# Row work of an attention kernel cut into four pieces, four more row maxima in its lead-in, and first rows on two queues

## The chip, the cores and the metric

One Trainium2 chip, one of its cores. The metric is the device time of one execution in microseconds (us). The engines are named as in the profile: PE (TensorE, the matmuls), PEld (TensorE's weight loads), DVE (VectorE), ACT (ScalarE), POOL (GpSimd) and SP (SyncE, which issues most DMAs).

## The reference

The input x has 2048 rows of 512. It is normalized, goes through multi-query attention (32 heads of 16 that share one k and one v) and, beside that, through two dense layers with Mish between them; the result is x plus their gated product.

```python
xn = _layernorm(x, axis=-1)
q = (xn @ wq).reshape(B, S, H, Dh).transpose(0, 2, 1, 3)      # S = 2048, H = 32, Dh = 16
k, v = xn @ wk, xn @ wv                                       # one key and value head
p = softmax(einsum("bhqd,bkd->bhqk", q, k) * Dh ** -0.5)
s = einsum("bhqk,bkd->bhqd", p, v).reshape(B, S, H * Dh) @ wo
h = einsum("bsd,df->bsf", xn, w1) + b1                        # F = 1792
g = silu(einsum("bsf,fd->bsd", h * tanh(softplus(h)), w2))
return x + s * g
```

## The kernel before, in words

**Steps.** The attention is 32 groups (v) of queries and heads, each against 16 blocks of 128 keys: 512 steps, step s being block s % 16 of group s // 16. A step makes four score products (`e`, L1090), four exponentials of them on ScalarE (`pts`, L1095) and, two steps later, eight products of these with the values into the bank `pv` (L1176). Since the softmax subtracts each query's maximum, a step also makes four products `m` (L1118) of a later group's queries, the other way round, so that VectorE can take their maxima along the free axis (L1122, into the table `mb`). These run LEAD = 20 steps ahead; 64 of them, 32 for each of two sides (a = 0 and 1), make up a group. The last 20 steps have none, and are run in ten pairs (`tail_pair`).

**Row work.** When both sides' counters `m_next` have reached `m_need(v)`, that is 32 * (v + 1), `top_rows` takes up the row work of group v, which `c_rows` (L1134) defines as four functions: `reduce` (L1141, the maximum over the four key chunks), `parts` (L1144 and L1146, the maximum's split into two numbers), `turn` (L1153, four transposes of 32 by 32) and `move` (two DMAs, L1162). These bring the maxima as two more rows into the queries' tile `qt`, where the score products of step 16 v and later read them. The functions stand in a queue, `rowq`, as three pieces: reduce, parts, turn with move. After each step `top_rows(1)` takes one piece; after a step that evacuated a bank on VectorE (`evacs[0]`) none, after each half of a unit two, after a pair three.

**Dense work.** PE's remaining time goes to the projections and the two dense layers, group by group: 12 or so accumulating products into a bank `xps`, each cut into two half-height products (L122) of which one side runs beside the other side's attention products. In `waves` (L619) a step takes k = 6, 4 or 8 of them, or none; below these are called w6, w4, w8 and w0 steps. A group of 13 to 16 products runs as a unit (`unit`, L684): four steps in two halves, each half with 16 half products, eight e, eight m and two steps' pv products (16). `unit_ready` opens one only at a step divisible by 4, and only when each item that the group reads is ready by the planner's clock; for a weight that comes last it grants a slack, `g.most`, of 0.5 steps there and of 2 elsewhere. Weights arrive by DMA and are split by POOL into a high and a low part (`wbs`, L170 and L175). The order on every engine is fixed when the program is built, from such estimates; at run time the engines only wait on semaphores.

**Banks.** In PSUM `e` has three banks, `m` three, `pv` one and `xps` one.

**Lead-in.** Before step 0, a planner loop (L1453 to L1575) places load, normalization, projections and the first maxima as tasks with estimated costs. It makes 2 * LEAD = 40 maxima per side, then group 0's row work, whose DMAs set `cdone`, the time at which the rows are expected in `qt`. Until 0.4 us before that time PE is given dense products, or, where no group is ready, products that nobody reads (`keep_warm`, L1431).

Of the kernel before, what the change touches and what calls it, by code (L numbers as in the profile page):

```python
# [20 lines left out]
P = 128  # L21
# [12 lines left out]
LEAD = 20  # L34
# [94 lines left out]
def block_kernel(ctx: ExitStack, tc: tile.TileContext, x, wq, wk, wv, wo, w1, b1, w2, out):  # L129
# [1004 lines left out]
    def c_rows(v):  # L1134

        mp = sb.tile([P, 2, 3, 8], F32R, tag="mp", name=f"mp{v}", bufs=2)
        mx = f(mp[:, :, 0])
        w = {}

        def reduce():  # L1140
            dve.reduce_max(out=mx, in_=mb_of[v].rearrange("p b (a z) -> p a z b", a=2), axis=AX.X)  # L1141

        def parts():
            dve.tensor_reduce(out=mp[:, :, 1], in_=mx.rearrange("p a (z o) -> p a z o", o=1), axis=AX.X,  # L1144
                              op=ALU.max, negate=True)
            dve.tensor_reduce(out=f(mp[:, :, 2]), in_=f(mp[:, :, 0:2]).rearrange("p a s z -> p a z s"), axis=AX.X,  # L1146
                              op=ALU.add, negate=True)

        def turn():
            cr = w["cr"] = sb.tile([32, P], F32, tag="cr", name=f"cr{v}", bufs=2)  # L1150
            for b in range(4):
                z = slice(32 * b, 32 * b + 32)
                dve.transpose(cr[:, z], f(mp[z, :, 1:3]).rearrange("p a s z -> p a (s z)"))  # L1153

        def move():
            q, cr = qt_of[v], w["cr"]
            if not lead:
                sp_t[0] = max(sp_t[0], us_of(step[0]) + 4.0)
            for a in range(1, -1, -1):
                r = 64 * a + 48  # L1160
                sp_at(0.68)
                sp.dma_start(f(q[r:r + 2]).rearrange("o p (t n) -> o (p t) n", n=P), cr[16 * a:16 * a + 16])  # L1162
        return reduce, parts, turn, move

    def pv(s):
# [268 lines left out]
    pick = [None, None]  # L1434

    def m_ready(t):
        if min(m_next) >= 2 * LEAD:
            return None

        def ready(v, n, a):  # L1440
            i = 2 * (n % 8 // 4) + a
            if len(qready.get(v) or ()) <= i or n // 8 not in kready:
                return 1e9
            return max(t, qready[v][i], kready[n // 8][a])
        r = []
        if m_next[0] == m_next[1]:
            free = m_ends[(-3, -5)[len(mseq) % 2] if 15 in xp_of else -2]
            s = [max(free, *(ready(v, got[v], a) for a in range(2))) if got[v] < 32 else 1e9 for v in range(2)]
            v = int(s[1] + 0.6 < s[0])
            r.append((s[v], (0, 1), (v, got[v])))  # L1450
        else:
            e = mseq[m_next[1]]
            r.append((max(ready(*e, 1), m_ends[-3]), (1,), e))  # L1453
        if m_next[0] < 4:
            r.append((max(ready(0, got[0], 0), m_ends[-3]) + 0.05, (0,), (0, got[0])))
        z, pick[0], pick[1] = min(r, key=lambda z: z[0])
        return z if z < 1e8 else None
# [17 lines left out]
    while True:  # L1475
# [19 lines left out]
        if not any(o[1] == "ACT" and o[0] < T["ACT"] + 0.1 for o in opts):  # L1495
            opts.append((T["ACT"], "ACT", "J"))
        s, e, k = min(opts, key=lambda o: o[0])
        if cdone[0] is not None and s >= cdone[0] - 0.4 and min(m_next) >= 2 * LEAD:
            break
        when(s)  # L1500
        for tag in items:
# [1 line left out]
        if k == "M":  # L1503
            d = max(T["DVE"], s + 0.45)
            for a in pick[0]:
                if m_next[a] == len(mseq):
                    mseq.append(pick[1])
                    got[pick[1][0]] += 1
                m_one(a)
                d += 0.6  # L1510
                m_ends.append(d)
            T["DVE"] = d
            T["PE"] = s + (0.25 if kind[0] == "M" else 0.45)
            kind[0] = "M"
            if vdone[0] == 0 and got[0] == 32 and m_next[0] == m_next[1]:
                vdone[0] = 1
                r = c_rows(0)
                r1 = task("DVE", 1.2, lambda: (r[0](), r[1](), r[2]()))

                def move():  # L1520
                    r[3]()
                    cdone[0] = now[0] + 2 * 0.65 + 2.0
                task("SP", 1.3, move, [r1])
        elif k == "X":
            fresh = cur["g"] is None
            if cur["g"] is not None or not waiting and (vdone[0] or begun[0] < 1 + (s - 18) / X_US) and begin():
                begun[0] += fresh
                fill(3)
                T["PE"] = s + 0.23 * 3 + (0.2 if kind[0] == "M" else 0)
                kind[0] = "X"  # L1530
            else:
                keep_warm()
                T["PE"] = s + 0.25
                kind[0] = "X"
        elif k == "J":
            tag = next((g for g in ("wq", "ws", "wb") if not any(soon(k, s) for k in plan["POOL"]) and arrived(g) and busy[0] + E0 < s + (4.5 if g == "ws" else 0.5)), None)
            n = ran[0]
            if tag:
                split(tag)
                T["ACT"] = s + 0.6  # L1540
            else:
                gap[0] = 0
                if not plan["POOL"]:
                    act_jobs(1)
                T["ACT"] = s + (0.65 if ran[0] > n else 0.15)
        else:
            plan[e].remove(k)
            if k.fill and cur["g"] is not None and s < 27.0:
                fill(1)
            elif k.fill and cur["g"] is None and not waiting:  # L1550
                keep_warm()
            k.fn()
            T[e] = max(s, T[e]) + k.us + (0.15 if e == "PE" and kind[0] == "M" else 0)
            k.end = T[e]
            if e == "PE":
                kind[0] = "T"
# [9 lines left out]
    rowq = deque()  # L1566
    skip = [0]

    def top_rows(n):
        if vdone[0] < 8 * NC and min(m_next) >= m_need(vdone[0]):  # L1570
            r = c_rows(vdone[0])
            rowq.extend([r[0], r[1], lambda r=r: (r[2](), r[3]())])
            vdone[0] += 1
        for _ in range(min(n, len(rowq))):
            rowq.popleft()()  # L1575

    def unit_ready(s):
        if cur["g"] is not None or cur["chunk"]:
            return False
        for g in queue:  # L1580
            g.most = 0.5
        due(s)
        ok = begin()
        for g in queue:
# [89 lines left out]
    for s in range(NS + 2000):  # L1674
        inm = s < NS - LEAD
        if s < skip[0]:
            continue
        if s % 4 == 0 and s + 4 <= NS - LEAD and unit_ready(s):
            for h in range(2):
                unit(s, h)  # L1680
                top_rows(2)
                evacs[0] = 0
                pump()
            base[:] = s + 4, us_of(s) + UNIT_US
# [2 lines left out]
        if inm or cur["chunk"]:  # L1687
# [2 lines left out]
            h = s % 2  # L1690

            def em(k):
                n = m_sides(1 - h, k // 2) if inm else 0
                x = deque(lambda i=i: e_one(s, i) for i in range(4))
                y = deque(lambda: m_one(1 - h) for _ in range(n))
                r = [[], []]
                for op in FEW if k == 4 else EM:
                    if op == "M" and y:
                        r[1 - h].append(y.popleft())
                    elif op == "E":  # L1700
                        r[1 - h].append(x.popleft())
                r[h] = [lambda: m_one(h) for _ in range(4 - n if inm else 0)]
                return r

            if s >= 2 and (s - 1) % 16 == 0 and s > 1:
# [8 lines left out]
        elif TAIL <= s < NS:  # L1714
            due(s)
            tail_pair(s)
            top_rows(3)
            evacs[0] = 0
            base[:] = s + 2, us_of(s) + PAIR_US
            pump()  # L1720
# [11 lines left out]
            due(s + 0.5)  # L1732
            fill(16)
        step[0] = s
        top_rows(0 if evacs[0] else 1)
        evacs[0] = 0
        base[:] = s + 1, us_of(s) + K_US.get(halves[0], STEP_US)
        pump()
# [14 lines left out]
```

## Time and profile before

| | |
|---|---|
| median of 3 runs | 1565.14 us (1565.11 to 1565.82) |
| the profiled execution | 1565.04 us, of which its span 1563.2 us |
| PE busy | 1551.0 us, 99% |
| DVE busy | 1366.9 us, 87% |
| ACT busy | 1295.0 us, 83% |
| POOL busy | 637.8 us, 41% |
| granted TensorE clock | 1.00 over the span |

The profile shows one execution. The span runs from its first to its last recorded instruction; the execution's time is 1.8 us longer. A busy share is an engine's busy time over the span: it does not tell what the engine that is behind waits for, which the chain of waits does.

### The profile page before, as it was taken

The numbers are of one execution on the slowest core, as the hardware profiler recorded it, in microseconds if no ns is written. First come the engines' busy times: TensorE is split into PE (matmuls) and PEld (weight loads), VectorE is DVE, ScalarE is ACT, GpSimd is POOL, SyncE is SP. The second block draws the span as 40 slices with busy tenths as digits, with TensorE's granted clock in tenths as the row PEclk, the third lists the DMA queues.
The fourth block names the chain that finished last, engine by engine and source line by source line (L and its number), as shares of the span: only waits on it lengthen the run. The fifth ranks groups of instructions, "written<-read, shape, count | busy, mean of one in ns | idle before, by whom it ended". The sixth has DMA issues, their size and how long they took to land.

```text
span 1563.2 us, 31137 instructions
## 1 busy us (share of the span) xinstructions
PE 1551.0 (99%) x11722; PEld 862.5 (55%) x11722; DVE 1366.9 (87%) x2376; ACT 1295.0 (83%) x2509; POOL 637.8 (41%) x668
## 2 busy tenths in 40 slices
PE   9999999999999999999999999999999999999998
PEld 6545655555455565565555556556554555565654
DVE  7988888888989988898999998898889999889945
ACT  6599888779888788877989788798798887879786
POOL 5788339437348121440543424054044232404213
PEclk9999999999999999999999999999999999999999
DMA  6343123224131313112214231222321223121021
GB/s 205 110 140 125 39 85 127 68 85 139 59 120 56 105 32 112 58 33 91 64 31 139 78 93 30 76 81 86 97 60 32 87 69 111 31 86 45 8 75 42
DMA packets 68498, 125.46 MB, mean 80 GB/s; under 512 B 15262, under 2 KB 29900, under 8 KB 68348
## 3 DMA queue, kind: packets, MB, share of 16 engines
q1 hardware_dynamic: 67916, 122.68, 24.7%
q8 instruction: 93, 1.52, 0.4%
q10 hardware_dynamic: 432, 0.79, 0.1%
q14 instruction: 57, 0.47, 0.1%
HBM read 75.57 MB, written 26.21 MB: 65 GB/s over the span
## 4 chain that ended last, share of the span: by engine, by line
PE 97%; DVE 2%; ACT 1%; DMA 0%; issue 0%; SPq 0%; DVEq 0%
PE xps L122 44%; PE pv L1176 32%; PE m L1118 11%; PE e L1090 6%; PE xps L118 1%; DVE mb L1122 1%; PE wop L122 0%; PE kp L356 0%; PE xp L315 0%; DMA pts<-in_dram 0%; ACT pts L1095 0%; PE y2ps L122 0%; PE warm L1431 0%; PE wop L118 0%; DVE cr L1153 0%
## 5 line engine op out<-in xcount | busy, mean ns | idle before, releaser
L1122 DVE TENSOR_REDUCE mb<-m 128x1 f32<-128x512 f32 x2048 | 1265.6, 682 | 152.2 <-PE m L1118 118.3
L1095 ACT ACTIVATE pts<-e 128x512 f32<-128x512 f32 x2048 | 1065.6, 605 | 220.1 <-PE e L1090 162.4
L1118 PE MATMUL m<-ks,qt 48*128 48x512 f32 (+1 forms) x2048 | 846.1, 424 | 1.7 <-DVE mb L1122 1.4
L1090 PE MATMUL e<-qt,ks 64*128 64x512 f32 x2048 | 752.1, 407 | 0.4 <-ACT pts L1095 0.4
L1176 PE MATMUL pv<-pts,vaug 128*32 128x512 f32 x4096 | 530.1, 603 | 0.0
L1118 PEld LDWEIGHTS m<-ks,qt 48*128 48x128 f32 (+1 forms) x2048 | 371.3, 185 | 91.3 <-DVE mb L1122 54.0
L1090 PEld LDWEIGHTS e<-qt,ks 64*128 64x128 f32 x2048 | 376.0, 186 | 26.7 <-ACT pts L1095 12.9
L122 PE MATMUL xps<-wbs,act 64*128 64x512 f32 x1270 | 324.0, 399 | 0.1
L122 PE MATMUL xps<-xt,ws 64*128 64x512 f32 x1128 | 312.3, 409 | 1.0 <-ACT pts L1095 1.0
L122 PEld LDWEIGHTS xps<-xt,ws 64*128 64x128 f32 x1128 | 194.3, 185 | 184.9 <-ACT pts L1095 123.2
L122 PEld LDWEIGHTS xps<-wbs,act 64*128 64x128 f32 x1270 | 227.3, 184 | 97.2 <-ACT pts L1095 26.8
L1176 PEld LDWEIGHTS pv<-pts,vaug 128*32 128x32 f32 x4096 | 88.1, 108 | 151.5 <-issue 143.9
L185 POOL TENSOR_SCALAR t<-t 128x512 f32<-128x512 f32 x56 | 34.5, 616 | 274.3 <-ACT t L814 274.3
L175 POOL TENSOR_TENSOR hb<-hb,t 128x512 f32<-128x512 f32 x56 | 72.2, 1289 | 120.7 <-ACT t L827 76.0
L122 PE MATMUL xps<-xt,wq 64*128 64x512 f32 x336 | 93.1, 409 | 0.0
L122 PEld LDWEIGHTS xps<-xt,wq 64*128 64x128 f32 x336 | 57.9, 185 | 55.0 <-ACT pts L1095 36.9
L122 PE MATMUL xps<-wbs,ot_all 64*128 64x512 f32 x288 | 79.4, 408 | 0.0
L122 PEld LDWEIGHTS xps<-wbs,ot_all 64*128 64x128 f32 x288 | 49.5, 184 | 47.1 <-ACT pts L1095 28.5
L175 POOL TENSOR_TENSOR act<-hb,act 128x512 fp32r<-128x512 f32 x56 | 72.2, 1290 | 4.7
L175 POOL TENSOR_TENSOR hb<-hb,u 128x512 f32<-128x512 f32 x56 | 72.3, 1292 | 4.4
L175 POOL TENSOR_TENSOR u<-u,t 128x512 f32<-128x512 f32 x56 | 72.0, 1286 | 4.7
L175 POOL TENSOR_TENSOR oc<-oc,sc 128x512 f32<-128x512 f32 (+1 forms) x16 | 20.6, 1288 | 113.6 <-ACT sc L1204 56.3
(164 smaller groups left out, 900.8 us busy)
## 6 DMA issues: line engine op xcount, KB each, us to landing
wbs<-w SPq DMA_DIRECT2D x39, 512.0 KB
ws<-w SPq DMA_DIRECT2D x36, 512.0 KB
qt<-qh SPq DMA_DIRECT2D x256, 32.0 KB
w<-wbs SPq DMA_DIRECT2D x14, 512.0 KB
wq<-wq SPq DMA_DIRECT2D x14, 512.0 KB
wbs<-wo SPq DMA_DIRECT2D x12, 512.0 KB
rawws<-in_dram SPq DMA_DIRECT2D x20, 256.0 KB
w<-ws SPq DMA_DIRECT2D x10, 512.0 KB
```

Source lines behind the costliest of these rows:

```text
L118: self.pe.matmul(ps, self.lhs(), self.rhs(), start=(self.k == 0), stop=(self.k == self.tot - 1))
L122: i = self.pe.matmul(ps, self.lhs()[o], self.rhs()[o], start=(self.k == 0 and self.halves == 0), stop=(self.k == self.tot - 1 and self.hal ...
L175: eng.tensor_tensor(out=o, in0=a, in1=b, op=op)
L185: pool.tensor_scalar(o, o, lim, 0.0, op0=ALU.min, op1=ALU.max)
L1090: pe.matmul(e, ks[o:o + 64, P * k:P * (k + 1)], q[o:o + 64, p], start=True, stop=True)
L1095: x = act.activation(dst, e, AF.Exp, scale=0.25)
L1118: pe.matmul(m, q[o, p, P * t:P * (t + 1)], ks[o, C * kb:C * (kb + 1)], start=True, stop=True)
L1122: return dve.reduce_max(out=mb_of[v][:, kb, z:z + 1], in_=m, axis=AX.X)
L1176: pe.matmul(o[32 * j:32 * j + 32], vaug[:, k], pt, start=(k == 0), stop=(k == 15))
```

## The change

- The lead-in makes 42 maxima per side in place of 40 (84 in all). As each step still makes four, the table is one step further on throughout, and the last step that has maxima is 490 in place of 491.
- `turn` is cut in two, `turn(0)` and `turn(1)`, of two transposes each. The pieces of group v get due steps: reduce 16 v - 6, parts 16 v - 5, turn(0) 16 v - 4, turn(1) with move 16 v - 3. `top_rows` issues every piece whose step has come, so several at once where the group is taken up late; steps that evacuate are no longer left out, and one rule (`ends`) draws a piece forward by a step.
- Of group 0's two row DMAs the second, of side 0, is issued by ACT's queue and no longer by SP's.
- The lead-in's loop ends 2.5 us before the expected landing when no group is ready and the 84 maxima are placed, where it placed unread products before.
- `unit_ready` grants a slack of 1.5 in place of 0.5. A unit needs eight maxima on each side to be left, where it needed to end before the tail.

```diff
-        def turn():
-            cr = w["cr"] = sb.tile([32, P], F32, tag="cr", name=f"cr{v}", bufs=2)
-            for b in range(4):
+        def turn(n):
+            if n == 0:
+                w["cr"] = sb.tile([32, P], F32, tag="cr", name=f"cr{v}", bufs=2)
+            for b in range(2 * n, 2 * n + 2):
                 z = slice(32 * b, 32 * b + 32)
-                dve.transpose(cr[:, z], f(mp[z, :, 1:3]).rearrange("p a s z -> p a (s z)"))
+                dve.transpose(w["cr"][:, z], f(mp[z, :, 1:3]).rearrange("p a s z -> p a (s z)"))
...
                 sp_at(0.68)
-                sp.dma_start(f(q[r:r + 2]).rearrange("o p (t n) -> o (p t) n", n=P), cr[16 * a:16 * a + 16])
+                (act if lead and a == 0 else sp).dma_start(f(q[r:r + 2]).rearrange("o p (t n) -> o (p t) n", n=P), cr[16 * a:16 * a + 16])
...
     def m_ready(t):
-        if min(m_next) >= 2 * LEAD:
+        if min(m_next) >= 2 * LEAD + 2:
             return None
...
-        if cdone[0] is not None and s >= cdone[0] - 0.4 and min(m_next) >= 2 * LEAD:
+        if cdone[0] is not None and s >= cdone[0] - 0.4 and min(m_next) >= 2 * LEAD + 2:
             break
...
-                    cdone[0] = now[0] + 2 * 0.65 + 2.0
-                task("SP", 1.3, move, [r1])
+                    cdone[0] = now[0] + 0.75 + 1.9
+                task("SP", 0.7, move, [r1])
...
+            elif cdone[0] is not None and s > cdone[0] - 2.5 and min(m_next) >= 2 * LEAD + 2:
+                break
             else:
                 keep_warm()
...
-    def top_rows(n):
+    def top_rows(s, n):
+
         if vdone[0] < 8 * NC and min(m_next) >= m_need(vdone[0]):
-            r = c_rows(vdone[0])
-            rowq.extend([r[0], r[1], lambda r=r: (r[2](), r[3]())])
+            v = vdone[0]
+            r = c_rows(v)
+            rowq.extend((16 * v - 6 + k, fn) for k, fn in enumerate(
+                (r[0], r[1], lambda: r[2](0), lambda: (r[2](1), r[3]()))))
             vdone[0] += 1
-        for _ in range(min(n, len(rowq))):
-            rowq.popleft()()
+        g = cur["g"]
+        ends = n == 1 and s % 4 == 2 and g is not None and g.dve and not cur["chunk"]
+        while rowq and (rowq[0][0] <= s or ends and rowq[0][0] == s + 1):
+            rowq.popleft()[1]()
...
-            g.most = 0.5
+            g.most = 1.5
...
-        if s % 4 == 0 and s + 4 <= NS - LEAD and unit_ready(s):
+        if s % 4 == 0 and max(m_next) + 8 <= 32 * NU and unit_ready(s):
             for h in range(2):
                 unit(s, h)
-                top_rows(2)
+                top_rows(s + 2 * h + 1, 2)
...
-        top_rows(0 if evacs[0] else 1)
+        top_rows(s, 1)
```

**VectorE, group 6, in w6 steps.** Here `mb_4131` (before) and `mb_4038` (now) hold group 6's maxima, the other `mb` group 7's; `mp` and `cr` are the row work's tiles, and `m_1_4` is maximum product 4 of side 1. Before:

```order
L1141 TENSOR_REDUCE mp_4763<-mb_4131 128x2x8
L1122 TENSOR_REDUCE mb_4769<-m_1_0_4770 128x1
L1122 TENSOR_REDUCE mb_4769<-m_1_1_4778 128x1
L1122 TENSOR_REDUCE mb_4769<-m_1_2_4786 128x1
L1122 TENSOR_REDUCE mb_4769<-m_0_0_4793 128x1
L1144 TENSOR_REDUCE mp_4763<-mp_4763 128x2x8
L1146 TENSOR_REDUCE mp_4763<-mp_4763 128x2x8
L1122 TENSOR_REDUCE mb_4769<-m_0_1_4807 128x1
L1122 TENSOR_REDUCE mb_4769<-m_0_2_4815 128x1
L1122 TENSOR_REDUCE mb_4769<-m_0_3_4823 128x1
L1122 TENSOR_REDUCE mb_4769<-m_1_3_4830 128x1
L1153 STREAM_TRANSPOSE cr_4845<-mp_4763 32x32 x4
```

Now:

```order
L1141 TENSOR_REDUCE mp_4775<-mb_4038 128x2x8
L1144 TENSOR_REDUCE mp_4775<-mp_4775 128x2x8
L1146 TENSOR_REDUCE mp_4775<-mp_4775 128x2x8
L1122 TENSOR_REDUCE mb_4716<-m_1_2_4783 128x1
L1122 TENSOR_REDUCE mb_4716<-m_1_3_4791 128x1
L1122 TENSOR_REDUCE mb_4716<-m_1_4_4799 128x1
L1122 TENSOR_REDUCE mb_4716<-m_0_2_4806 128x1
L1154 STREAM_TRANSPOSE cr_4817<-mp_4775 32x32 x2
L1122 TENSOR_REDUCE mb_4716<-m_0_3_4821 128x1
L1122 TENSOR_REDUCE mb_4716<-m_0_4_4829 128x1
L1122 TENSOR_REDUCE mb_4716<-m_0_5_4837 128x1
L1122 TENSOR_REDUCE mb_4716<-m_1_5_4844 128x1
```

The two remaining transposes are the row that follows. Reduce and parts, which stood four maxima apart, now stand together: after step 16 v - 6 one side of the group was still one maximum short, so it was taken up after 16 v - 5, when both pieces were due. The four transposes, which stood together, stand four maxima apart. So stands the row work of 15 groups (1, 4, 6, 8, 9, 10, 12, 15, 17, 18, 21, 23, 26, 27, 29); of the others groups 7 and 25 alone have four pieces after four steps.

**VectorE, group 2, at the unit of steps 28 to 31.** `mb_1461` and `mb_1397` are group 2's maxima. Before:

```order
L1141 TENSOR_REDUCE mp_2130<-mb_1461 128x2x8
L1122 TENSOR_REDUCE mb_2136<-m_1_0_2137 128x1
L1122 TENSOR_REDUCE mb_2136<-m_1_1_2145 128x1
L1122 TENSOR_REDUCE mb_2136<-m_1_2_2153 128x1
L1122 TENSOR_REDUCE mb_2136<-m_1_3_2161 128x1
L1122 TENSOR_REDUCE mb_2136<-m_1_4_2172 128x1
L1122 TENSOR_REDUCE mb_2136<-m_1_5_2184 128x1
L1122 TENSOR_REDUCE mb_2136<-m_1_6_2191 128x1
L1122 TENSOR_REDUCE mb_2136<-m_1_7_2198 128x1
L1144 TENSOR_REDUCE mp_2130<-mp_2130 128x2x8
L1146 TENSOR_REDUCE mp_2130<-mp_2130 128x2x8
L1153 STREAM_TRANSPOSE cr_2219<-mp_2130 32x32 x4
```

Now:

```order
L1141 TENSOR_REDUCE mp_2137<-mb_1397 128x2x8
L1144 TENSOR_REDUCE mp_2137<-mp_2137 128x2x8
L1146 TENSOR_REDUCE mp_2137<-mp_2137 128x2x8
L1122 TENSOR_REDUCE mb_2079<-m_1_2_2145 128x1
L1122 TENSOR_REDUCE mb_2079<-m_1_3_2153 128x1
L1122 TENSOR_REDUCE mb_2079<-m_1_4_2161 128x1
L1122 TENSOR_REDUCE mb_2079<-m_1_5_2169 128x1
L1122 TENSOR_REDUCE mb_2079<-m_1_6_2180 128x1
L1122 TENSOR_REDUCE mb_2079<-m_1_7_2192 128x1
L1122 TENSOR_REDUCE mb_2079<-m_1_8_2199 128x1
L1122 TENSOR_REDUCE mb_2079<-m_1_9_2206 128x1
L1154 STREAM_TRANSPOSE cr_2225<-mp_2137 32x32 x4
```

Reduce alone stood ahead of the eight maxima of the unit's first half, and now parts stand there with it. After the half, parts and four transposes have become the four transposes. So it is in seven groups (2, 13, 14, 19, 20, 22, 28).

**PE, steps 68 to 71.** `act_5` to `act_10` are tiles of the hidden layer, here the left operand of a second-layer group whose right operand is `wbs`. Before, in step 70:

```order
L122 MATMUL xps<-wbs,act_9_2203 128x512
L1090 MATMUL e_6_1_1_3895<-qt_78,ks 128x512
L122 MATMUL xps<-wbs,act_9_2203 128x512
L1118 MATMUL m_1_22_3899<-ks,qt_79 128x512 [waits DVE_49]
L122 MATMUL xps<-wbs,act_9_2203 128x512
L1090 MATMUL e_7_0_1_3903<-qt_78,ks 128x512
L122 MATMUL xps<-wbs,act_10_3232 128x512 [waits Pool_49]
L1118 MATMUL m_1_23_3907<-ks,qt_79 128x512 [waits DVE_49]
L122 MATMUL xps<-wbs,act_10_3232 128x512 [waits Pool_49]
L1090 MATMUL e_7_1_1_3911<-qt_78,ks 128x512 [waits Activation_49]
L1176 MATMUL pv_3741<-pts,vaug 32x512 x4
```

Now, at the end of the first half of a unit of steps 68 to 71:

```order
L122 MATMUL xps<-wbs,act_9_2372 128x512
L1118 MATMUL m_1_23_3858<-ks,qt_79 128x512 [waits DVE_49]
L122 MATMUL xps<-wbs,act_9_2372 128x512
L1090 MATMUL e_7_0_1_3862<-qt_78,ks 128x512 [waits Activation_49]
L122 MATMUL xps<-wbs,act_9_2372 128x512
L1118 MATMUL m_1_24_3865<-ks,qt_79 128x512 [waits DVE_49]
L122 MATMUL xps<-wbs,act_10_3243 128x512 [waits Pool_49]
L1090 MATMUL e_7_1_1_3869<-qt_78,ks 128x512 [waits Activation_49]
L122 MATMUL xps<-wbs,act_10_3243 128x512 [waits Pool_49]
L1118 MATMUL m_1_25_3872<-ks,qt_79 128x512 [waits DVE_49]
L1177 MATMUL pv_3752<-pts,vaug 32x512 x8
```

The group's last two products wait for POOL (they read the last weight tile that it splits) and stood in the third of four w8 steps; they now stand ahead of sixteen pv products at the end of the first half. This is the one unit that is added (31 before, 32 now), and the four w8 steps are gone.

**PE, end of the lead-in.** `xtw`, `ws_842` and `ws_929` are projection weights. Before:

```order
L118 MATMUL xps<-xt_175,xtw 128x512 x6
L118 MATMUL xps<-xt_175,ws_842 128x512 x12
L1431 MATMUL warm<-qt_79 128x512 x2
L122 MATMUL xps<-xt_175,ws_929 128x512
L1118 MATMUL m_1_8_980<-ks,qt_78 128x512
L122 MATMUL xps<-xt_175,ws_929 128x512
L1090 MATMUL e_0_0_1_984<-qt_77,ks 128x512
L122 MATMUL xps<-xt_175,ws_929 128x512
L1118 MATMUL m_1_9_988<-ks,qt_78 128x512
L122 MATMUL xps<-xt_175,ws_929 128x512
```

Now:

```order
L118 MATMUL xps<-xt_175,xtw 128x512 x6
L118 MATMUL xps<-xt_175,ws_842 128x512 x6
L1118 MATMUL m_0_8_961<-ks,qt_78 128x512
L1118 MATMUL m_1_8_964<-ks,qt_78 128x512
L1118 MATMUL m_0_9_969<-ks,qt_78 128x512
L1118 MATMUL m_1_9_972<-ks,qt_78 128x512
L118 MATMUL xps<-xt_175,ws_842 128x512 x3
L122 MATMUL xps<-xt_175,ws_842 128x512
L1118 MATMUL m_1_10_982<-ks,qt_78 128x512
L122 MATMUL xps<-xt_175,ws_842 128x512
L1090 MATMUL e_0_0_1_986<-qt_77,ks 128x512
L122 MATMUL xps<-xt_175,ws_842 128x512
```

The two `warm` products are gone, four maximum products stand there, and the last three of a group's twelve full products have become half products of the first two steps. Four steps without dense products (8 to 11) have become two (2 and 3) and two with three half products (0 and 1). From step 12 to 67 the dense work lies as before.

## Rows read from the trace of the kernel before

Each line of the chain and of an engine's list is: start us, duration us, what.

**Rows 1.** Page: granted clock in 40 slices, and the chain's shares by engine.
```profile
PEclk9999999999999999999999999999999999999999
...
PE 97%; DVE 2%; ACT 1%; DMA 0%; issue 0%; SPq 0%; DVEq 0%
```
**Rows 2.** Chain of waits in order of time, steps 93 to 95 (w6).
```profile
347.30 1.00 PE pv L1176 x8
...
350.16 0.99 PE pv L1176 x8
...
353.14 1.00 PE pv L1176 x8
```
**Rows 3.** VectorE in order of time, the same steps (group 6's parts and turn).
```profile
348.35 0.16 DVE L1144 TENSOR_REDUCE mp<-mp 128x16 fp32r<-128x16 f32 x1
...
348.79 2.48 DVE L1122 TENSOR_REDUCE mb<-m 128x1 f32<-128x512 f32 x4
351.19 0.83 DVE L1153 STREAM_TRANSPOSE cr<-mp 32x32 f32<-32x32 f32 x4
351.96 2.43 DVE L1122 TENSOR_REDUCE mb<-m 128x1 f32<-128x512 f32 x4
```
**Rows 4.** VectorE in order of time, unit of steps 476 to 479, first half.
```profile
1455.60 0.27 DVE L1141 TENSOR_REDUCE mp<-mb 128x16 f32<-128x64 f32 x1
...
1456.21 4.86 DVE L1122 TENSOR_REDUCE mb<-m 128x1 f32<-128x512 f32 x8
```
**Rows 5.** Chain of waits, units of steps 472 to 475 and 476 to 479.
```profile
1447.64 1.85 PE pv L1176 x16
...
1453.59 1.85 PE pv L1176 x16
...
1459.82 1.85 PE pv L1176 x16
```
**Rows 6.** Chain of waits, first half of the unit of steps 28 to 31.
```profile
156.73 1.03 PE pv L1176 x8
...
161.88 1.85 PE pv L1176 x16
```
**Rows 7.** Chain of waits, steps 253 (w6), 254 and 255 (w4).
```profile
809.35 0.99 PE pv L1176 x8
...
815.20 1.00 PE pv L1176 x8
...
817.91 1.00 PE pv L1176 x8
```
**Rows 8.** PE in order of time, end of the first half at step 28.
```profile
161.28 0.39 PE L122 MATMUL xps<-wbs,act 64*128 64x512 f32 x1
161.40 0.49 PE L1118 MATMUL m<-ks,qt 48*128 48x512 f32 x1
```
**Rows 9.** POOL in order of time, the split that makes step 70's last weight tile.
```profile
278.25 1.31 POOL L175 TENSOR_TENSOR wbs<-rawwb,wbs 128x512 fp32r<-128x512 f32 x1
```
**Rows 10.** Chain of waits, steps 68 to 73 (four w8 steps, then a unit's first half).
```profile
273.33 1.00 PE pv L1176 x8
...
279.45 0.99 PE pv L1176 x8
...
282.51 0.99 PE pv L1176 x8
...
290.83 1.85 PE pv L1176 x16
```
**Rows 11.** Chain of waits from the lead-in's end into the first steps.
```profile
72.61 3.07 PE xps L118 x12
...
76.45 0.51 PE warm L1431
...
77.80 2.06 ACT pts L1095 x4
```
**Rows 12.** ScalarE in order of time there; in brackets the idle time before and its releaser.
```profile
75.71 0.69 ACT L808 ACTIVATE hb<-xps,b1c 128x512 f32<-128x512 f32 x1 [2.02 <-PE xps L118]
```

More of the change, by code (lines that the diff above doesn't have):

```diff
@@ L1517, in block_kernel @@
                 r = c_rows(0)
-                r1 = task("DVE", 1.2, lambda: (r[0](), r[1](), r[2]()))
+                r1 = task("DVE", 1.3, lambda: (r[0](), r[1](), r[2](0), r[2](1)))
                 def move():
                     r[3]()
-                    cdone[0] = now[0] + 2 * 0.65 + 2.0
-                task("SP", 1.3, move, [r1])
+                    cdone[0] = now[0] + 0.75 + 1.9
+                task("SP", 0.7, move, [r1])
         elif k == "X":
@@ L1692, in em @@
             def em(k):
-                n = m_sides(1 - h, k // 2) if inm else 0
+                tops = inm and min(m_next) < 32 * NU
+                n = m_sides(1 - h, k // 2) if tops else 0
                 x = deque(lambda i=i: e_one(s, i) for i in range(4))
@@ L1701, in em @@
                         r[1 - h].append(x.popleft())
-                r[h] = [lambda: m_one(h) for _ in range(4 - n if inm else 0)]
+                r[h] = [lambda: m_one(h) for _ in range(4 - n if tops else 0)]
                 return r
@@ L1716, in block_kernel @@
             tail_pair(s)
-            top_rows(3)
+            top_rows(s + 1, 2)
             evacs[0] = 0
```

## The prediction

> **What bounds the kernel now.** I read the page first, then the chain of waits, then single engines in order of time at the places that the change moves. PE carries 97% of the chain that ended last [rows 1], so time comes only from PE doing less or waiting less. The chain also dates the steps: step s ends with a block of eight pv products, so the distance from one block to the next is a step. A w6 step with no more than the two operations of parts on VectorE takes 350.16 - 347.30 = 2.86 us; the next, behind the four transposes, 353.14 - 350.16 = 2.98 [rows 2]. VectorE shows why. The four maxima of a step take 2.48 [rows 3], which leaves some 0.37 of the 2.86. Parts take 348.79 - 348.35 = 0.44 up to the next maximum and cost PE nothing, as VectorE had reached its gap early; the transposes take 351.96 - 351.19 = 0.77, the next four maxima start late, and the last m product waits for one of its three banks. So a whole turn costs 0.12 in a w6 step, and a row job of up to 0.44 costs nothing.
>
> **Row work, as the order now has it.** The change says four pieces over four steps. The order does so in two groups (7 and 25). In most, the group is taken up one step late, and reduce and parts come out together, then two transposes, then two. No operation is added or removed, so only stalls count.
>
> In w6 steps (15 groups) a turn of 0.77 in one gap becomes reduce with parts in one gap and two half turns of about 0.39 in two. The nearest row for the joined piece is at the unit of step 476, where it stands already: 1456.21 - 1455.60 = 0.61 [rows 4]. Half turns lie under the free 0.44, so they cost nothing. The joined piece of 0.61 lies between free (0.44) and 0.12 (0.77). I take 0.12, so no gain: it starts where the turn started, ends only 0.16 earlier, and still exceeds the gap by more than parts do. The ends are -0.12 each (-1.8) and 0.
>
> In first halves of units (seven groups) reduce alone becomes reduce with parts. Plain, a half takes 1453.59 - 1447.64 = 5.95; the one with both takes 1459.82 - 1453.59 = 6.23 [rows 5]. With reduce alone it takes 161.88 - 156.73 = 5.15 behind a single step [rows 6]; behind a block of sixteen it would be 1.85 - 0.99 = 0.86 more, 6.01. So the change pays 6.23 - 6.01 = 0.22 in each, 7 x 0.22 = +1.54. What left there, parts ahead of the second half's transposes, stood beside sixteen pv products and cost nothing. The ends are -0.06 (even reduce becomes free) and +0.62 (the third rival).
>
> In groups 16 and 24 the turn stood in a w4 step: steps 253 and 254 take 815.20 - 809.35 = 5.85, against 2.86 and a plain w4 step of 817.91 - 815.20 = 2.71 [rows 7], 0.28 lost. Now the joined piece stands in a w6 step at 0.12: 2 x -0.16 = -0.32. Group 3 loses its turn's stall, -0.12. Groups 7 and 25 would lose theirs too, but their parts now follow a bank's evacuation by VectorE; I take 0 for both. Rows together: **+1.1**.
>
> The Trainium skill (VectorE: DVE Perf Modes, section The DRAIN you can't avoid) says that a VectorE operation does not start until the one before has left the pipe; with maxima that end to end would fill the step, any cut of the row work would cost the same, the row term would be 0 and the time 1565.4. The trace does not agree: four maxima in 2.48 start before their forerunners end, as the next one's start at 351.96, ahead of the transposes' end at 351.19 + 0.83 = 352.02, also shows [rows 3].
>
> **The unit at step 68.** The slack of 1.5 lets a unit replace four w8 steps. Each of these takes 282.51 - 279.45 = 3.06 [rows 10], four 12.24; a unit takes 2 x 5.95 = 11.90, so -0.34. The first half of the unit that follows now takes (290.83 - 282.51) - 3.06 = 5.26 [rows 10], 0.17 over the plain 5.95 - 0.86 = 5.09, as an evacuation by VectorE delays it; between two units, as at 476, that falls under the pv products: -0.17. Against that, the last two products need a weight tile that POOL finishes at 278.25 + 1.31 = 279.56 [rows 9]. A unit's last half product starts 161.28 - 156.73 = 4.55 after the pv block that opens it [rows 6, 8]; opened at 273.33 [rows 10] it would start at 277.88. PE waits 279.56 - 277.88 = 1.68, with sixteen pv products queued behind, and the next e and m behind those; ScalarE and VectorE have their inputs early by nothing like that. Ends: 0 (the tile comes earlier) and +1.7. I take the whole, since neither POOL's nor the weight DMA's place in the order has moved there. Unit together: **+1.2**.
>
> **Lead-in.** The last group's twelve full products take 3.07 from 72.61, an unread product follows at 76.45 for 0.51, and the first exponential starts at 77.80 [rows 11]. Now nine of the twelve stay (2.30), four maximum products come in, which I put at 0.7 (two sides run beside each other), and the first steps start at 72.61 + 3.0 = 75.6 in place of 76.96, 1.35 earlier. The first steps are ScalarE's, which runs without a break from 77.80. The evacuation of 0.69 that stood in its idle time, ahead of the unread product [rows 12], now falls among the exponentials. So -1.35 + 0.69, about **-0.7**. The ends are -1.35 (the evacuation finds a hole) and +1.0 (each maximum product waits 0.60 for VectorE, so that PE starts 0.3 late, and the evacuation counts as well). The row DMA that moves to ACT's queue is issued in ScalarE's wait of 2.02 [rows 12], before anything else there has its input: 0, and without that cover its wait for the transposes would hold the evacuation behind it. SP's queue is freed by one issue, which nothing there waits for. The unread products themselves cost only where the path runs through them, which is counted.
>
> **Tail.** The last step with maxima loses four m products. Two half products are worth 2.86 - 2.71 = 0.15, so at most 0.3; the exponentials set the tail, and I take **-0.1**.
>
> **Sum.** 1.1 + 1.2 - 0.7 - 0.1 = +1.5 on the profiled 1565.04, which lies 0.10 under the median of the runs: 1566.5. A measurement can tell about 0.2% (3.1 us) from no change, so this is no change.
>
> **Rivals.**
> - *The joined piece doesn't stall.* For it: it is 0.16 shorter than a turn, and parts at 0.44 are free. Against: the unit at 476 shows it stalling. Then 15 x -0.12, 7 x -0.06, 2 x -0.28 and 3 x -0.12 give -3.1 for the rows, 4.2 less: 1562.3. Chance 0.15.
> - *The unit finds its weights.* If the tile's DMA or split comes 1.7 earlier, the 1.68 falls away: 1564.8. Against it is POOL's unmoved order. Chance 0.11. Both of these: 1560.6, chance 0.05.
> - *Slower: the seven halves pay more.* VectorE's eight maxima take 4.86 of a half [rows 4], so it can hardly catch up, and an m product that has waited takes 0.49 where one that flows takes 0.39 [rows 8]. If four more products in each restart, that is 7 x 0.4 = 2.8 more: 1569.3. It decides from about 0.26 more per half (6.49 in place of 6.23), where the time passes 1568.3. For it: the half with both pieces would be followed by a lagging second one; against: the half at 476 already contains such restarts and takes 6.23. Chance 0.11.
> - *Slower: the clock.* The granted clock is full in all slices [rows 1], also while unread products ran. If it fell to 1.2 of 2.4 GHz where they are gone, two steps could take up to 2.86 more each: 1572.2. Against it: four maximum products stand in their place, so PE is not idle longer. The Trainium skill (TensorE: Matmul & The Clock Gate, Part 1: The HAM clock gate) says that the clock is released by PE's recent activity and throttled after idleness; this trace shows no fall. Chance 0.03.
>
> **How the numbers follow.** My own case, with all four terms near what I took, has 0.55. Below 1562.0 lie the double rival (0.05) and the lower part of the first (0.06): faster 0.11. Above 1568.3 lie the third (0.11), the clock (0.03) and the upper bounds of the lead-in (0.02): slower 0.16. The rest, 0.73, is no change. The range 1562.0 to 1569.2 leaves out the double rival, part of the first, the clock and the far half of the third, together under 0.2. My own case alone would span 1565.2 to 1568.
>
> **What would show it.** In the changed profile, w6 steps that hold reduce and parts should take about 2.98 and those with two transposes 2.86; first halves of the seven units about 6.23 behind a unit; the unit at 68 should show a wait of PE of some 1.7 ahead of its last half products, ended by POOL, in its first half; the first exponential should start near 76.4, and step 12 lie about 0.7 earlier. Plain w6 steps on both sides of a joined piece would make the row term wrong, a first half of the unit at 68 below 6 the unit term, and a first exponential after 77.5 the lead-in.

## The result and the profile after

The changed kernel takes 1567.73 us (median of 22 runs, 1566.19 to 1569.24) against 1565.39 (22 runs, 1564.72 to 1565.91): a ratio of 1.0015, 95% interval 1.0009 to 1.0022. That is 2.3 us slower, clear of 1 but less than the 0.2% that the prediction called no change, and inside its range; 1566.5 was forecast. One thing was not forecast: the changed kernel's runs spread over 3.05 us, those of before over 1.2. The mean granted clock of each run goes with it: the three runs at 1.000 took 1566.19 to 1566.45, the twelve at 0.998 or less 1567.72 to 1569.24.

The profiled execution took 1568.54 us, in the upper part of that spread. Its page (the span; TensorE's share of the chain; the products of the second layer, with the idle time before them and its releaser):

```profile
span 1566.7 us, 31152 instructions
...
PE 93%; POOL 3%; DVE 2%; ACT 1%; DMA 0%; issue 0%; POOLq 0%
...
L122 PE MATMUL xps<-wbs,act 64*128 64x512 f32 x1270 | 324.9, 399 | 1.2 <-POOL wbs L175 0.9
```

Where PE had 97% of the chain [rows 1], POOL now has 3%, and the second layer's products wait 0.9 for POOL's split. The distances between pv blocks, step by step, place the whole difference. In the table the first steps end at the block with the pv products of step 11 (it closes step 13, since pv runs two steps late), the rows are steps 16 v - 8 to 16 v + 1 of each group v from step 14 on, and the unit is what lies between groups 4 and 5. The table is of one profile each, and first steps vary: `old_lead_in` below, with the lead-in of before, shows +0.8 there.

| last pv block against before, us (rounded) | predicted | changed, profiled |
|---|---|---|
| rows | +1.1 | +0.4 |
| unit at step 68 | +1.2 | +1.3 |
| lead-in and first steps | -0.7 | +1.8 |
| tail and the rest | -0.1 | -0.1 |
| sum | +1.5 | +3.5 |

**The first steps.** Stretches of 2 us of the changed kernel, with the columns stretch, length, PE busy (products), PEld, DVE, ACT, POOL, then granted clock, DMA share and GB/s:

```profile
80.00:82.00 2.00, 1.52 (x6) 0.69 (x6) 2.00 (x4) 2.00 (x5) 1.83 (x3) 1.00 0.68 275
82.00:84.00 2.00, 1.94 (x7) 0.87 (x7) 2.00 (x4) 2.00 (x5) 1.92 (x3) 0.69 0.00 0
84.00:86.00 2.00, 2.00 (x9) 0.32 (x9) 0.73 (x2) 1.78 (x4) 2.00 (x2) 0.50 0.00 0
86.00:88.00 2.00, 2.00 (x10) 0.83 (x6) 0.74 (x2) 0.71 (x2) 1.83 (x3) 0.50 0.45 131
88.00:90.00 2.00, 2.00 (x12) 0.49 (x10) 1.74 (x3) 1.46 (x3) 1.92 (x3) 0.60 0.00 0
90.00:92.00 2.00, 2.00 (x18) 1.39 (x14) 1.31 (x3) 1.08 (x3) 1.83 (x4) 1.00 0.17 48
```

The granted clock falls to 0.50, the lower of its two levels, in steps 2 and 3, behind a stretch in which PE had six products and was idle a quarter of the time. Idle time alone doesn't mark it: the kernel before was as idle here, with twice the products, and kept its clock.

```profile
78.00:80.00 2.00, 1.52 (x12) 1.00 (x10) 2.00 (x5) 2.00 (x5) 0.00 (x0) 1.00 1.02 385
80.00:82.00 2.00, 1.51 (x14) 1.06 (x10) 2.00 (x5) 2.00 (x5) 1.46 (x2) 1.00 0.61 247
```

The clock row of the changed kernel's page, in 40 slices of 39 us each, still shows a 9 everywhere; only short stretches show the fall. In those, ACT and DVE, full up to 84, then have holes: now PE sets the pace. The chain of the changed kernel:

```profile
76.86 0.60 ACT pts L1095
...
80.75 0.58 ACT hb L808
...
84.63 1.86 PE pv L1177 x8
...
88.80 1.39 PE pv L1177 x8
```

The first exponential starts 0.94 earlier than before [rows 11], the evacuation `hb` stands among the exponentials as the prediction had it, and the first pv block still came at 84.6, as before. Then it took 1.86, where an undisturbed block of eight takes 1.00 [rows 2].

**The unit at step 68.** PE in order of time, and the chain that led to it:

```profile
279.82 0.49 PE L122 MATMUL xps<-wbs,act 64*128 64x512 f32 x1 [0.30 <-POOL wbs L170]
...
281.18 0.49 PE L122 MATMUL xps<-wbs,act 64*128 64x512 f32 x1 [0.87 <-POOL wbs L175]
...
281.62 1.92 PE L1177 MATMUL pv<-pts,vaug 128*32 128x512 f32 x16
```

```profile
276.04 3.02 DMA rawwb<-in_dram
...
279.85 1.29 POOL wbs L175
```

The last two half products wait for POOL, sixteen pv products stand behind them, as forecast. The first half took 6.7 us; the prediction's plain half of 5.09 with its wait of 1.68 is 6.8.

**The rows.** VectorE at the joined piece: group 4 (step 60), group 6 (step 92), group 10 (step 156).

```profile
253.13 0.27 DVE L1141 TENSOR_REDUCE mp<-mb 128x16 f32<-128x64 f32 x1
...
253.74 2.48 DVE L1122 TENSOR_REDUCE mb<-m 128x1 f32<-128x512 f32 x4
...
348.16 0.25 DVE L1141 TENSOR_REDUCE mp<-mb 128x16 f32<-128x64 f32 x1
...
348.76 2.47 DVE L1122 TENSOR_REDUCE mb<-m 128x1 f32<-128x512 f32 x4
...
530.27 0.68 DVE L175 TENSOR_TENSOR y<-xps,y 128x512 f32<-128x512 f32 x1
530.87 1.28 DVE L1122 TENSOR_REDUCE mb<-m 128x1 f32<-128x512 f32 x2
532.07 0.26 DVE L1141 TENSOR_REDUCE mp<-mb 128x16 f32<-128x64 f32 x1
...
532.66 2.48 DVE L1122 TENSOR_REDUCE mb<-m 128x1 f32<-128x512 f32 x4
```

PE's pv blocks at both ends of steps 60 and 92:

```profile
251.89 1.07 PE L1177 MATMUL pv<-pts,vaug 128*32 128x512 f32 x8
...
254.90 1.06 PE L1177 MATMUL pv<-pts,vaug 128*32 128x512 f32 x8
...
347.05 1.06 PE L1177 MATMUL pv<-pts,vaug 128*32 128x512 f32 x8
...
349.92 1.06 PE L1177 MATMUL pv<-pts,vaug 128*32 128x512 f32 x8
```

The piece takes 0.60 each time. In group 4 its step took 3.01 (2.84 before); in group 6 reduce started 0.13 earlier after its step's beginning, and the step took 2.87. Steps with half a turn take 2.85, as forecast. In group 10 the piece comes on top of an evacuation (`y`), since the new `top_rows` no longer leaves such steps out: 3.48 in place of 2.88.

### The profile page after: what moved, and what is told of

Its sections match the earlier page's. It is cut to its first block, busy times and chain, and to the rows that moved or that the text cites. A ratio compares the mean times of both kernels' runs of the same rounds, so it can differ in the third digit from the quotient of the medians.

```text
span 1566.7 us, 31152 instructions
## 1 busy us (share of the span) xinstructions
PE 1555.4 (99%) x11723; PEld 864.0 (55%) x11723; DVE 1364.9 (87%) x2376; ACT 1295.2 (83%) x2509; POOL 636.7 (41%) x668
## 3 DMA queue, kind: packets, MB, share of 16 engines
q8 instruction: 93, 1.52, 0.4%
## 4 chain that ended last, share of the span: by engine, by line
PE 93%; POOL 3%; DVE 2%; ACT 1%; DMA 0%; issue 0%; POOLq 0%
PE xps L122 43%; PE pv L1177 30%; PE m L1118 10%; PE e L1090 6%; DVE mb L1122 2%; PE xps L118 1%; ACT pts L1095 1%; PE warm L1345 1%; POOL hb L175 0%; PE kp L356 0%; PE xp L315 0%; DMA rawwb<-in_dram 0%; PE wop L122 0%; POOL xt L175 0%; POOL u L175 0%
```

## The experiments

The theory after the result: (C) the first steps lose because PE has so little to do in steps 2 and 3 that the clock falls, in some runs longer than in others; the unit costs its wait; the rows cost what is joined. The rival for the first steps (A): ScalarE sets them, and the slow clock only fills PE's waiting time. Ratios are to runs of the kernel before made beside each experiment (medians 1565.56 to 1565.66).

**Real work in steps 2 and 3.**

```diff
-        if ... cur["g"] is None and (step[0] % 4 or not begin())):
+        if ... cur["g"] is None and (step[0] % 4 and step[0] != 2 or not begin())):
```

> The changed kernel, but the next group of dense products may begin at step 2 as well as at steps divisible by 4: steps 2 and 3 get six half products each, and steps 6 and 7 have none instead. Theory C (the clock): the changed kernel loses in its first steps because PE has so little to do in steps 2 and 3 that its granted clock falls to 0.50 around 83 to 89 us, by an amount that differs from run to run; with dense products there the clock stays at 1.00, step 12 comes 1.5 to 2.5 us earlier than in the changed kernel's profile, the median is about 1566.2 us (the changed kernel's fastest runs), and the runs lie within 1.3 us of each other. Theory A (ScalarE sets the first steps, and the slow clock only fills time in which PE would wait): 1567.2 to 1568.2, whatever the clock does.

Measured: 1566.07 us (11 runs, 1565.59 to 1566.51), ratio to before 1.0003 (0.9994 to 1.0011). The spread is gone, and the clock holds through the stretches where it fell:

```profile
82.00:84.00 2.00, 1.67 (x11) 0.70 (x11) 2.00 (x4) 2.00 (x6) 1.92 (x3) 1.00 0.00 0
84.00:86.00 2.00, 2.00 (x20) 1.15 (x13) 0.93 (x3) 1.73 (x5) 1.91 (x3) 1.00 0.15 40
```

The pv block of step 11 lies 3.15 before the changed kernel's, more than the 1.5 to 2.5 expected. ScalarE has the same work. But the dense products that steps 2 and 3 gain are taken from steps 6 and 7, so not all of the 3.15 need be the clock; `new_lead_in_alone` below, which moves none, parts the two. Over all runs the fall goes with the thin steps: no run of this kernel or of `dense_from_step2_slack_0_5` (22) has a mean clock under 0.999, while 12 of 22 of the changed kernel, 6 of 11 of `new_lead_in_alone` and 8 of 11 of `slack_0_5` have 0.998 or less.

**Unread work there.** Products into an unread bank, meant as six in step 2 and six in step 3. The trace shows six in all, from 82.3 to 85.2, in step 2 alone:

```diff
+        spare = ps_x.tile([P, C], F32, tag="x", name="spare") if new and not mms and step[0] in (1, 2) else None
...
+                if spare is not None and pairs > 1:
+                    for _ in range(2):
+                        pe.matmul(spare, qts[2][:, 0, 0:P], qts[2][:, 0], start=True, stop=True)
```

> The changed kernel, with six products that nobody reads in step 2 and six in step 3, between the maximum products and the scores from the second pair on. Theory C: the clock stays at 1.00 and the median is about 1566.2 us with runs within 1.3 us, though PE does more. Theory A: added work on PE in steps that ScalarE sets is neutral at best, 1567.5 to 1568.5 us. If the clock falls all the same, the cause of the fall lies before step 2.

Measured: 1569.82 us (6 runs, 1568.44 to 1573.20), a miss by 3.6. In the profile the clock stays at 1.00 in the first steps, and step 11 lies 1.25 before the changed kernel's. That shows little for theory C: step 3 got no work, and the first steps of `new_lead_in_alone` kept their clock without any, 1.1 earlier still. The miss comes from the unit at 68, which now costs 4.1 in place of 1.3:

```profile
280.00:282.00 2.00, 1.13 (x8) 0.34 (x10) 0.27 (x1) 0.11 (x1) 1.92 (x3) 1.00 0.93 263
282.00:284.00 2.00, 2.00 (x16) 0.35 (x8) 0.42 (x1) 1.06 (x2) 1.84 (x3) 0.57 0.81 298
284.00:286.00 2.00, 2.00 (x12) 1.19 (x10) 0.58 (x1) 0.15 (x2) 1.09 (x1) 0.58 0.65 244
```

```profile
279.79 0.50 PE L122 MATMUL xps<-wbs,act 64*128 64x512 f32 x1 [1.50 <-POOL wbs L170]
...
281.17 0.49 PE L122 MATMUL xps<-wbs,act 64*128 64x512 f32 x1 [0.87 <-POOL wbs L175]
...
281.60 3.04 PE L1183 MATMUL pv<-pts,vaug 128*32 128x512 f32 x16
```

Its weight's DMA took 4.22 from issue to release in the chain (3.02 in the changed kernel), so PE waited 1.50 and 0.87 for the two parts of the split, and behind that the clock fell, which it had not done in the first steps. So a wait can cost more than itself: the sixteen pv products behind it took 3.04 in place of 1.92. PE's being earlier is not enough for it: in `dense_from_step2`, 1.9 earlier still, that DMA took 3.09 and the unit cost 1.4. Why the DMA took longer here is open. The step that failed was to price the unit as a constant.

**The old lead-in under the new rows.**

```diff
-        if min(m_next) >= 2 * LEAD + 2:
+        if min(m_next) >= 2 * LEAD:
...
-            elif cdone[0] is not None and s > cdone[0] - 2.5 and min(m_next) >= 2 * LEAD + 2:
-                break
```

> The changed kernel with the lead-in of before: 80 maxima, both first row DMAs on SP's queue, unread products to its end. Row pieces and the unit at step 68 stay as changed. Theory C: no fall of the clock, so only the rows (+0.5) and the unit (+1.3) are left over before: about 1567.2 us, with runs within 1.3 us of each other in place of the changed kernel's 3. Theory A gives the same median if the lead-in costs ScalarE 0.5, but does not foretell a narrower spread. If the spread stays at 3 us, it comes from the rows or the unit.

Measured: 1570.45 us (6 runs, 1570.10 to 1570.61), a miss by 3.2 with the narrow spread that was expected. Rows took +3.4 here, not +0.5, the unit +1.2, the first steps +0.8 in the profile. With 80 maxima a group's last maximum stands directly ahead of its reduce:

```profile
347.42 0.27 DVE L1141 TENSOR_REDUCE mp<-mb 128x16 f32<-128x64 f32 x1
...
348.02 2.48 DVE L1122 TENSOR_REDUCE mb<-m 128x1 f32<-128x512 f32 x4
```

There group 6's step takes 3.01 like group 4's; every joined piece in a w6 step pays some 0.15 or more, and those behind an evacuation 0.73. So the four extra maxima were worth some 3 us to the row work, a benefit that the prediction didn't see: with them, three maxima of the next group stand between a group's last one and its reduce.

**The new lead-in alone**, under the old rows and the old slack (the diff of the lead-in, applied to the kernel before).

> The kernel before with the changed lead-in alone (84 maxima, the second first-row DMA on ACT's queue, no unread products at the end); rows in three pieces and four w8 steps at 68 as before. Theory C: the granted clock falls to about half for some us between 80 and 92, the median is 1565.4 to 1566.6 us, and the runs spread by some 3 us. The prediction's term for the lead-in taken by itself: 1564.7 us and a narrow spread.

Measured: 1565.39 us (11 runs, 1563.95 to 1567.08), ratio 0.9999 (0.9991 to 1.0008). The spread of 3.1 comes with the lead-in alone. The profiled run took 1564.04, near the lower end, and its clock is 1.00 where the changed kernel's fell, though its PE has the same six products from 80 to 82:

```profile
80.00:82.00 2.00, 1.50 (x6) 0.61 (x6) 2.00 (x4) 2.00 (x5) 1.83 (x3) 1.00 0.59 214
82.00:84.00 2.00, 1.62 (x7) 0.71 (x5) 2.00 (x5) 2.00 (x6) 1.92 (x3) 1.00 0.20 82
...
115.62 1.07 PE L1176 MATMUL pv<-pts,vaug 128*32 128x512 f32 x8
```

The last line is the block of step 11; in the changed kernel's trace it is this one:

```profile
118.00 1.07 PE L1177 MATMUL pv<-pts,vaug 128*32 128x512 f32 x8
```

So the profile doesn't show the fall that was expected, but the runs do: the six with a mean clock of 0.998 took 1565.39 to 1567.08, the five with more 1563.95 to 1564.97. What decides it in one run and not in another, no profile here tells. The two profiles are the best measure of the clock's price: up to that block, but for group 1's row work, both kernels have the same work, ScalarE's included, and with the fall the block starts 2.4 later. So A falls.

**The old slack.**

```diff
-            g.most = 1.5
+            g.most = 0.5
```

> The changed kernel with the old slack of 0.5, so that steps 68 to 71 are four w8 steps again. Theory: the unit there costs what its wait for the split weight tile costs (1.3 us between the two profiles), so the median is 1566.4 us; since this kernel still loses a varying amount in its first steps, the runs still spread by some 3 us. Rival (the wait at the unit only takes up a lead that PE has over the weights, and the same wait falls due later): 1567.4 to 1568 us.

Measured: 1567.37 us (11 runs, 1565.15 to 1568.11). In its profile the unit's term is +0.05 (four w8 steps), but its clock fell too, some 0.8 later than the changed kernel's and for as long, and the first steps took +2.1. The spread covers the difference, so this run alone doesn't decide. The same edit on the kernel with dense products in steps 2 and 3 does:

> The kernel of dense_from_step2 with the old slack of 0.5: the unit at step 68 by itself, in a kernel whose clock holds. Theory: the unit cost 1.3 us, so 1564.8 us against the 1566.07 of dense_from_step2, with runs within 1.3 us; what is left against the kernel before is the rows (+0.5) and a lead-in that gains 1.0 to 1.3 as the prediction meant it to. Rival (the unit's wait only takes up a lead over the weights): 1565.7 us or more.

Measured: 1564.91 us (11 runs, 1564.56 to 1565.83) against 1566.07: the unit cost 1.2, and it was not paid later.

**88 maxima**, so that each group is whole one step earlier and its pieces really stand in four steps.

In its three places:

```diff
-        if min(m_next) >= 2 * LEAD + 2:
+        if min(m_next) >= 2 * LEAD + 4:
...
```

> The changed kernel with 44 maxima per side in the lead-in in place of 42. Then both sides of a group are whole after step 16 v - 6, and the order has reduce, parts and two half turns after four different steps in nearly all groups; besides, the last projection group's twelve products all stand in the lead-in, and steps 0 to 3 have dense products. Theory: each piece by itself fits VectorE's gap, so w6 steps take 2.86 throughout and units' first halves 5.95 behind a unit; against the kernel before the rows gain 3.0, the unit costs 1.3, the first steps gain 0.5 to 1.0, and the clock stays at 1.00: 1563.2 us, with runs within 1.3 us. Rival (joined or not, row work of the same length spills by the same amount): 1566 us. Rival (four more maxima in the lead-in delay step 0, as VectorE takes 0.60 for each): 2.4 more, 1565.6 us.

Measured: 1564.82 us (11 runs, 1563.79 to 1567.06), 1.6 above the forecast. It lies between forecast and second rival: the rows gain 3.0 in its profile, as expected, the unit costs 1.3, but the first steps cost 1.2 in place of gaining. The spread of 3.3 is wider than expected; the clock is 1.00 in the profile of one run. The longest is the only one with a mean clock under 1.000 (0.999); where it fell is not known.

The same kernel with the old slack:

> The kernel of eighty_eight_maxima with the old slack of 0.5. Theory: the unit's 1.3 goes as well: 1561.9 us, 0.2% under the kernel before. If the unit's wait is eaten by an earlier PE (theory of a lead over the weights), it is the same as eighty_eight_maxima within 0.5.

Measured: 1563.58 us (11 runs, 1563.17 to 1564.43), ratio 0.9988 (0.9979 to 0.9997), 1.7 above the forecast. The slack is worth 1.2 here too. In the chain the first steps hang on VectorE, as the second rival for 88 maxima had it:

```profile
72.48 7.75 DVE mb L1122 x13
```

And that with both of the first row DMAs on SP's queue:

> The kernel of eighty_eight_and_slack_0_5 with both of the first row DMAs on SP's queue, as before. Theory: the first scores do not wait for the rows (PE arrives after they have landed), and ScalarE issues its DMA in idle time, so the queue is worth nothing: the same within 0.3 us. Rival (the second queue is what lets step 0 start earlier): 0.7 us more, one DMA issue on SP.

Measured: 1563.52 us (11 runs, 1563.24 to 1564.30): the second queue is worth nothing in that kernel.

**86 maxima**, the fewest with which both sides are whole after step 16 v - 6 (the last step with maxima then has two), and the old slack:

```diff
-        if min(m_next) >= 2 * LEAD + 2:
+        if min(m_next) >= 2 * LEAD + 3:
...
-            g.most = 1.5
+            g.most = 0.5
...
-                n = m_sides(1 - h, k // 2) if tops else 0
+                rest = min(4, 64 * NU - sum(m_next))
+                n = (m_sides(1 - h, k // 2) if rest == 4 else 32 * NU - m_next[1 - h]) if tops else 0
...
```

> The kernel of eighty_eight_and_slack_0_5 with 43 maxima per side in the lead-in in place of 44; the last step with maxima has two in place of four. After step 16 v - 6 each side of a group is still whole, so the pieces stay apart. Theory: with 88, VectorE's maxima set the start (the chain runs through 13 of them in a row, 7.75 us, up to the first steps); two fewer are 2 x 0.60 = 1.2 us less, the rest is the same: 1562.4 us, with runs within 1.3 us. Rival (with two fewer ScalarE sets the start, as in the changed kernel, and gives back only a part): 1562.9 to 1563.3 us.

Measured: 1562.16 us (11 runs, 1561.98 to 1563.19), ratio 0.9979 (0.9970 to 0.9988): 3.4 us under the kernel before and 5.6 under the changed one, with a clock of 1.00; 1562.4 was expected. Its rows gain 3.0, its unit 0, its first steps 0.1 in the profile. VectorE around group 6 shows the four pieces in four gaps, and no maximum of them late:

```profile
342.01 0.26 DVE L1141 TENSOR_REDUCE mp<-mb 128x16 f32<-128x64 f32 x1
342.33 2.48 DVE L1122 TENSOR_REDUCE mb<-m 128x1 f32<-128x512 f32 x4
344.74 0.16 DVE L1144 TENSOR_REDUCE mp<-mp 128x16 fp32r<-128x16 f32 x1
344.93 0.19 DVE L1146 TENSOR_REDUCE mp<-mp 128x16 f32<-128x32 f32 x1
345.18 2.48 DVE L1122 TENSOR_REDUCE mb<-m 128x1 f32<-128x512 f32 x4
347.59 0.40 DVE L1154 STREAM_TRANSPOSE cr<-mp 32x32 f32<-32x32 f32 x2
348.04 2.48 DVE L1122 TENSOR_REDUCE mb<-m 128x1 f32<-128x512 f32 x4
350.55 0.42 DVE L1154 STREAM_TRANSPOSE cr<-mp 32x32 f32<-32x32 f32 x2
350.90 2.48 DVE L1122 TENSOR_REDUCE mb<-m 128x1 f32<-128x512 f32 x4
```

The maxima start every 2.85 or 2.86 us here.

## Why the prediction was right, and where it was not

- **The unit: right.** 1.2 forecast; 1.3 in the profile, 1.2 by the two pairs of kernels that differ in the slack alone. The 0.17 that the prediction took off for the unit that follows lies in group 5's steps, which gain 0.32 here and 0.15 in `slack_0_5`; with it the profile's term is 1.2 too. The wait it named stands ahead of the half products it named, ended by POOL. What it didn't foresee is that the wait grows when the weight's DMA takes longer (4.22 in place of 3.02 in `unread_in_steps_2_3`), and that the clock can fall behind it.
- **Row work: right in its parts, the sum a little high** (+1.1 forecast, +0.4 in the profile). The seven unit halves were put at +1.54 and took +1.50. The third rival, restarts of m products in these halves, is thereby out; its 0.39 from [rows 8] is a half product of the dense work, not an m product that flows. The w6 groups, put at 0, took +0.2, but as a sum of several kinds: seven saved 0.11 to 0.15, as the first rival said (groups 6, 8, 15, 17, 23, 26, 27); groups 4, 9, 12, 21 and 29 came out near 0; group 1 saved 0.3; 10 and 18 lost 0.8 and 0.4 to evacuations. What was left at 0 without a word, groups 5, 11 and 30, gained 0.5 together, 0.17 of it the unit's. The bound of -0.12 on each joined piece was thus met by seven of the fifteen. Not all of the term is the cut's: under the old rows the new lead-in by itself (`new_lead_in_alone`) already moves it by -0.6 (groups 1, 5, 7, 30 and 31 gain, group 10 loses 0.33), which the prediction left out.
- **Half turns: right.** W6 steps with two transposes take 2.84 to 2.86.
- **Lead-in: wrong.** The step that failed is the term of -0.7, in that it took the clock to hold, with 0.03 given to a fall: it came out at +1.8 in the profile. The term itself measures at -0.6 where the clock holds (step 11 in the profile of `new_lead_in_alone`), and at -1.0 to -1.35 in the two kernels with dense products from step 2, which also take them from steps 6 and 7. The first exponential came at 76.86, not 76.4, but the kernel earned its lead. The clock rival had the mechanism, with the wrong place: it looked at the lead-in's end, where the unread products went and maximum products came. PE was thin behind that, in steps 2 and 3, which the order had shown without dense products. It argued that PE was not idle longer, and didn't count products per microsecond there. The rival's price, up to 2.86 for each of two steps, was an upper bound: in the profiles the fall costs 118.00 - 115.62 = 2.4 for both steps together.
- **That the change doesn't do what it says: right,** and worth more than the prediction saw. The forecast took the joined pieces as given; two maxima more make them the four pieces that were meant, and the rows then cost 3.4 us less than in the changed kernel.

The forecast of 1566.5 is close to the three runs whose clock held (1566.19 to 1566.45) and 1.2 under the median. It came that near the median by luck: the first steps' error (+2.5 in the profile; in the median +1.3, since 2.3 less the rows' 0.4 and the unit's 1.3 leaves +0.6) stood against one of -0.7 in the rows.

The page of the Trainium skill that the clock rival named (TensorE: Matmul & The Clock Gate, Part 1: The HAM clock gate) says that idleness throttles the clock. The profile shows the fall, but not an idle engine ahead of it: PE was busy for 1.52 of 2 us, with six products, and in the kernel before a share of 1.51 to 1.52 went with 12 to 14 products and a clock of 1.00. So the busy share alone doesn't tell it here.

## What to carry to other kernels

When an edit moves work away from a stretch, ask how much TensorE still does there, not only who ends last: a stretch that another engine sets can take the clock down, and the steps behind it then run at half the clock. A spread of runs that grows from 1.2 to 3 us is a reason to set each run's mean granted clock beside its time, and then to look at the clock in stretches of 2 us, since 40 slices of the span hide it. An experiment's own trace should be read for what the edit did: `unread_in_steps_2_3` added six products where twelve were meant. And when pieces are given due times, look in the order whether they really come apart; a condition that is met one step late joins them again.

## What the runs showed of the hardware that was not expected

- The clock fell to 0.50 behind a stretch in which PE was busy for 1.52 of 2 us; PE's longest idle time in the nine us before was 0.30. It fell in another kernel (0.57 and 0.58 over two stretches) behind waits of 2.4 us in all for a weight tile, with PE busy for 0.49 and 1.13 of 2 us in the two stretches before it. In the same program it fell in some runs and hardly in others: mean clocks of the changed kernel's runs go from 1.000 to 0.997.
- The same load of a weight tile took 2.88 to 3.09 us from issue to release in `old_lead_in`, the changed kernel and `dense_from_step2`, and 4.22 in `unread_in_steps_2_3`.
- In the changed kernel's w6 steps reduce with parts takes 0.60 either way, but reduce starts 1.10 to 1.12 after its step's pv block in some groups and 1.22 to 1.24 in others, with the same instructions ahead of it in both (three maxima of the next group). That tenth goes with a step of 2.86 to 2.89 or of 3.00 to 3.01. Why it differs was not settled; with the group's own last maximum directly ahead (`old_lead_in`) it was never the earlier one.
